# Linear attention and a quick-GELU MLP on one core: the second weight chunk asked for ahead of the casts of k, a later gate, and turns of k moved behind output matmuls

## The chip, the cores and the metric

The kernel runs on one core of a Trainium2 chip. The metric is device time in microseconds (us) of one execution; smaller is better. Engines are named as in the profile: PE multiplies matrices, PEld loads its weights, DVE, ACT and POOL work elementwise, and SP only issues transfers. POOL issues transfers too, in line with its own elementwise work. Sixteen DMA engines carry all transfers.

## The reference

Attention comes first, with a decay `lam[h]` per head, over blocks of 64 positions; its output, with heads side by side, goes through an MLP:

```python
B, H, S, D = 4, 8, 768, 64
for b in range(S // 64):
    intra = einsum('bhic,bhjc->bhij', qb, kb) * Dmask       # lam ** (i - j), lower triangle
    out_b = einsum('bhij,bhjd->bhid', intra, vb) \
          + einsum('bhid,bhde->bhie', qb * lam_pow, kv_state)
    kv_state = lam ** 64 * kv_state + einsum('bhsd,bhse->bhde', kb * rev_pow, vb)
x = out.transpose(0, 2, 1, 3).reshape(3072, 512)
h = x @ w_in                                                # 512 x 2048
return (h / (1 + exp(-1.702 * h))) @ w_out                  # 2048 x 512
```

## The kernel before

The work is cut into six waves of 512 tokens. The first two waves (`w` = 0 and 1) take two batches each and 256 positions of each batch; the other four take all four batches and 128 positions of each. Inside the first two waves a batch is called `c` (0 or 1). This change lies wholly in the first wave, where nothing is in the memory of the core yet and every transfer is just arriving.

For one batch of the first wave the steps are these. `do_cast` (line 195) multiplies k or q, as loaded in float32, by powers of the decay and writes bfloat16; it works in two halves `g` of four heads, of two instructions each, on whichever engine it is given (line 204 of the profile). `turn_pe` (line 234) transposes a half on PE against an identity matrix (line 240) and copies the result out on ACT (line 223) or DVE (line 220). `cast_v` (line 225) casts v. `d_scores` (line 253) multiplies turned q and turned k (line 261), and the products are masked on DVE (line 269) into tiles named sm. `d_one` and `d_state` (line 281) make the running state from k that is not turned and v, `d_keep` (line 291) copies it out. `d_out` (line 310) makes the outputs: masked scores times v into two accumulators, oa and oz (line 318), then q times the state (line 300). `d_x` copies an accumulator to the MLP's input, xT. With xT there, `mlp1_half` (line 408) multiplies two column blocks of the input weight with the tokens of one batch (line 416), and `mlp1` (line 398) one column block with all tokens of the wave (line 404); both end in a GELU on ACT. `fill` issues matmuls of zeros, whose results nobody reads.

The input weight arrives in five chunks of 2, 3, 4, 4 and 3 column blocks of 128 (`IN_CH`, line 173). `load_w_in(j)` (line 180, issued at line 183) asks for chunk j on POOL's queue, converting float32 to bfloat16. In bfloat16 the chunks are 256, 384, 512, 512 and 384 KB. The output weight follows on the same queue in four chunks of 512 KB (`load_w_out`, line 187). The inputs k, q and v go on SP's queue instead (`load_one`, line 79): for batch 0 of the wave in two halves of four heads each, then batch 1 with k and q in halves and v in one piece.

The order of each engine's work is written out by hand: inside `tc.manual_schedule()` (line 686) every engine executes what the program gives it in program order. `gate_pool(x)` (line 680) is a copy of one element of x on POOL: whatever POOL has to do after it waits until x has landed.

The stretch that matters runs from line 695 to line 739: k and q of batch 0 are cast and turned; POOL passes its gate and asks for weight chunk 0; v of batch 0 is cast on ACT; scores of batch 0; POOL casts k of batch 1 and then asks for chunks 1 and 2; the state and output of batch 0 on PE, with the turns of k and q of batch 1 in between; scores of batch 1; the first MLP piece on chunk 0 (line 737), and the state of batch 1. Line 763 finishes batch 1, and the loop at line 764 runs the first MLP pieces that read chunk 1.

Of the kernel before, what the change touches and what calls it, by code (L numbers as in the profile page):

```python
# [25 lines left out]
def kernel(  # L26
# [16 lines left out]
    B, H, S, D = q.shape  # L43
# [33 lines left out]
    loaded = {}  # L77
# [61 lines left out]
    def acc(name, dt=f32, shape=None, tag="a"):  # L139
        return ps.tile(shape or [P, 4, P], dt, tag=tag, bufs={"a": 5, "mm": 3}[tag], name=name)  # L140

    def fill(n, new=None):
        if new:
            fill_ps[0] = acc("ps_fill", shape=[P, W], tag=new)
        for _ in range(n):
            nc.tensor.matmul(fill_ps[0], zero[:, 0:P], zero, start=True, stop=True)
# [33 lines left out]
    def load_w_in(j):  # L180
        c0 = sum(IN_CH[:j]) * P
        t, i = IN_HOME[j]
        nc.gpsimd.dma_start(
            out=w_in_sb[t][:, :, i * P : (i + IN_CH[j]) * P], in_=moe_w_in.rearrange("(kc ki) f -> ki kc f", ki=P)[:, :, c0 : c0 + IN_CH[j] * P])
# [10 lines left out]
    def do_cast(w, c, nm, eng, g=None):  # L195
        if g in (None, 0):
            cast[w, c, nm] = work.tile([P, 2, HD], bf16, tag=f"{nm}s{c}", bufs={"k": 2, "q": 1}[nm], name=f"{nm}s")
        f, x = loaded[w, c, nm], cast[w, c, nm]
        if w < ND:
            pw = {"k": kd_pow, "q": qd_pow}[nm]  # L200
            for R in (0, 1) if g is None else (g,):
                for j in range(2):
                    h = slice(4 * R + 2 * j, 4 * R + 2 * j + 2)
                    eng.tensor_tensor(x.rearrange("p a (r i j d) -> p r j i a d", i=2, j=2, d=D)[:, R, j],  # L204
                                      f[:, h].rearrange("p i (a d) -> p i a d", a=2),
                                      pw[:, h].unsqueeze(3).to_broadcast([P, 2, 2, D]), op=MUL)
        else:
            pw = {"k": k_pow, "q": q_pow}[nm]
            n = 2 * H // 4
            for j in range(2):  # L210
                eng.tensor_tensor(x.rearrange("p b (r i j d) -> p j (b r) i d", i=2, j=2, d=D)[:, j],  # L211
                                  f.rearrange("p h (a d) -> p (h a) d", a=2).rearrange("p (n j i) d -> p j n i d", j=2, i=2)[:, j],
                                  pw.rearrange("p b (r j i) -> p j (b r) i", i=2, j=2)[:, j].unsqueeze(3).to_broadcast([P, n, 2, D]),
                                  op=MUL)
# [10 lines left out]
    def cast_v(w, c, copies=(pool_copy, pool_copy)):  # L225
        f = loaded.pop((w, c, "v"))
        dst = v_sb[w % 2]
        if w < ND:
            for a in range(2):
                copies[a](dst[:, 2 * c + a], f.rearrange("p h (a d) -> p h a d", a=2)[:, :, a, :])  # L230
        else:
            copies[0](dst[:, 2 * c : 2 * c + 2].rearrange("p b h d -> p (b h d)"), f.rearrange("p h e -> p (h e)"))

    def turn_pe(w, c, nm, copy=act_copy, g=None):
        x = cast[w, c, nm]
        rr = list(range(NP)) if g is None else [2 * g, 2 * g + 1]
        t = acc("ps_t", bf16, [P, len(rr), 2, P])
        for i, r in enumerate(rr):
            for a in range(2):
                nc.tensor.transpose(t[:, i, a, :], x[:, a, r * P : (r + 1) * P], ident)  # L240
        if g in (None, 0):
            trans[w, c, nm] = work.tile([P, 2 * NP, P], bf16, tag=f"{nm}T{c}", bufs={"k": 1, "q": 2}[nm], name=f"{nm}T")
        copy(trans[w, c, nm][:, 2 * rr[0] : 2 * rr[0] + 2 * len(rr)], t.rearrange("p r a s -> p (r a) s"))
# [6 lines left out]
    def q_of(w, c, rows, r, blk):  # L250
        return trans[w, c, "q"][rows, 2 * r : 2 * r + 2, D * blk : D * blk + D]
# [34 lines left out]
    def d_one(w, c, tag="a"):  # L286
        states[w, c] = t = acc("ps_kv", shape=[P, NP, D], tag=tag)
        d_state(w, c, t, A)

    def d_keep(w, c):  # L290
        nc.scalar.copy(kv_sb[1][:, 2 * w + c], states[w, c])
        if w:
            kept[w, c] = work.tile([P, NP, D], f32, tag="half", bufs=1, name="half")
            nc.scalar.copy(kept[w, c], states[w, c])

    def d_inter(w, c, t, j, first):
        js, b = (A, Z)[j], 2 * w + c
        for R in range(2):
            for i, cs in enumerate((A, Z)):
                nc.tensor.matmul(t[cs, 2 * R + j, :], kv_sb[1][js, b, 2 * R + i, :], q_of(w, c, js, 2 * R + i, 1),  # L300
                                 start=(first and R == 0), stop=(not first), skip_group_check=True)
# [8 lines left out]
    def d_out(w, c, tags="aa"):  # L310
        vt = v_sb[w % 2]
        oa, old = acc("ps_o", tag=tags[0]), (w, c) in whole
        oz = whole.pop((w, c)) if old else acc("ps_o", tag=tags[1])
        for r in range(NP):
            for a in range(2):
                for t, bs in ((oa, A), (oz, Z)):
                    for i, cs in enumerate((A, Z)):
                        nc.tensor.matmul(t[cs, r, :], vt[bs, 2 * c + a, 2 * r + i, :],
                                         masked[w, c, r // 2, r % 2][bs, i, a, :],
                                         start=(r + a == 0 and (t is oa or not old)),  # L320
                                         stop=(a == 1 and (t is oa or (old and r % 2 == 0))), skip_group_check=True)
        d_inter(w, c, oz, 1, False)
        if w not in xT:
            xT[w] = xp.tile([P, NP, W], bf16, tag="x", name="xT")
        return oa, oz

    def d_x(w, c, i, t, copy):
        n0 = (2 * c + i) * P
        copy(xT[w][:, :, n0 : n0 + P], t)
# [350 lines left out]
    def gate_pool(x):  # L680
        nc.gpsimd.tensor_copy(behind_q, x)  # L681
# [4 lines left out]
    with tc.manual_schedule():  # L686
# [8 lines left out]
        for nm, copies in (("k", (dve_copy, act_copy)), ("q", (act_copy, dve_copy))):  # L695
            for g in range(2):
                do_cast(0, 0, nm, nc.vector, g)
            for g in range(2):
                turn_pe(0, 0, nm, copies[g], g)
                fill({"k0": 2, "q1": 1}.get(f"{nm}{g}", 0))  # L700
        gate_pool(loaded[0, 0, "v"][0:1, 0, 0:1])
        load_w_in(0)
        cast_v(0, 0, (act_copy, act_copy))
        d_scores(0, 0, 0)
        d_scores(0, 0, 1)
        fill(3)
        for g in range(2):
            do_cast(0, 1, "k", nc.gpsimd, g)
        for j in (1, 2):
            load_w_in(j)  # L710
        d_one(0, 0, "mm")
        d_keep(0, 0)
        turn_pe(0, 1, "k", act_copy, 0)
        oa, oz = d_out(0, 0, ("mm", "mm"))
        nc.scalar.copy(seen, oz[:, 3, P - 1 : P])
        d_state(0, 0, states[0, 0], Z)
        do_cast(0, 1, "q", nc.vector, 0)
        do_cast(0, 1, "q", nc.vector, 1)
        turn_pe(0, 1, "k", dve_copy, 1)
        d_x(0, 0, 0, oa, act_copy)  # L720
        turn_pe(0, 1, "q", act_copy, 0)
        d_inter(0, 0, oz, 0, False)
        turn_pe(0, 1, "q", dve_copy, 1)
        d_x(0, 0, 1, oz, act_copy)
        fill(1, "a")
# [164 lines left out]
```

## Time and profile before

| what | us |
|---|---|
| median of 3 runs | 193.13 |
| lowest and highest of the 3 | 191.82, 193.41 |
| the profiled execution, own time | 194.5 |
| its span, first to last instruction | 192.7 |
| PE busy in the span | 185.1 |
| DVE busy | 154.4 |
| ACT busy | 129.8 |
| POOL busy | 53.7 |

PE is busy for nearly all of the span, so what matters is where it is not, and where it runs at a lower clock. Times in the profile count from the first instruction. A row of the timeline reads: start, duration, engine, line, operation, output and inputs, count, and in brackets how long the engine sat idle before it and what ended that. The timeline merges instructions of one kind that follow one another. A row of the chain of waits reads: start, duration, what ran or was waited for. A row of the windows reads: from and to, length, then for each engine its busy time and number of instructions, the clock that PE was granted (1.00 is full), the mean busy share of the DMA engines (over 1 where packets overlap) and GB/s. The transfers of POOL's queue appear as q0, those of SP's as q1.

### The profile page before, as it was taken

What the parts mean: (1) busy time and instruction counts of PE and PEld (TensorE: products, weight loads), DVE (VectorE), ACT (ScalarE), POOL (GpSimd) and SP (SyncE); (2) the same over time, 40 slices, a digit from 0 to 9 for tenths busy, and PEclk for the clock granted to TensorE, in tenths of its full rate; (3) what the DMA queues carried; (4) which work ended last, traced back from release to release, by engine and by line L of the source; (5) the groups of instructions that cost most, each with busy time, mean ns of one, the idle gap of its engine ahead of it and who ended that gap; (6) DMA issues with size and microseconds to landing.
All of it is one profiled execution on the core that took longest, in us unless ns stands there. A gap on an engine that the chain in (4) does not pass through costs nothing.

```text
span 192.7 us, 5553 instructions
## 1 busy us (share of the span) xinstructions
PE 185.1 (96%) x2291; PEld 151.7 (79%) x2293; DVE 154.4 (80%) x296; ACT 129.8 (67%) x243; POOL 53.7 (28%) x78
## 2 busy tenths in 40 slices
PE   7796999999999999999999999999999999999993
PEld 2365644898888888888888888888888888888882
DVE  1896579987586989988799979799879797889850
ACT  4966376145869976479878388878388876587711
POOL 5299000059727000097000195000393000000000
PEclk9999699999999999999999999999999999999999
DMA  5999999999977698989998946999365903300113
GB/s 148 330 249 183 200 204 207 307 297 271 228 187 61 157 236 201 245 217 165 197 241 191 276 113 155 210 250 255 120 163 116 211 8 109 112 3 0 44 51 126
DMA packets 90495, 33.91 MB, mean 176 GB/s; under 512 B 67430, under 2 KB 90470, under 8 KB 90470
## 3 DMA queue, kind: packets, MB, share of 16 engines
q1 hardware_dynamic: 85716, 29.37, 62.2%
q0 software_dynamic: 4752, 4.19, 13.9%
q8 instruction: 18, 0.29, 0.7%
q14 instruction: 7, 0.06, 0.2%
q10 hardware_dynamic: 2, 0.00, 0.0%
HBM read 27.26 MB, written 6.29 MB: 174 GB/s over the span
## 4 chain that ended last, share of the span: by engine, by line
PE 89%; DMA 6%; SPq 2%; POOL 1%; issue 0%; ACT 0%; ACTq 0%; POOLq 0%
PE ps_X L463 18%; PE ps_hX L595 17%; PE ps_V L463 9%; PE ps_hV L595 9%; PE ps_h L404 5%; PE ps_Q L463 5%; PE ps_hQ L595 4%; PE ps_h L416 4%; PE ps_X L513 4%; DMA w_in<-in_moe_w_in_dram 4%; DMA kf<-in_k_dram 3%; PE ps_s L337 2%; PE ps_o L392 2%; SPq L84 2%; PE ps_o L379 1%; POOL ks L204 1%
## 5 line engine op out<-in xcount | busy, mean ns | idle before, releaser
L614 ACT ACTIVATE g_sb<-h_sb 128x512 bf16<-128x512 f32 x57 | 34.5, 632 | 1.2 <-DVE h_sb L603 1.2
L463 PEld LDWEIGHTS <-g_s 128*128 128x128 bf16 x320 | 30.9, 98 | 4.1
L595 PEld LDWEIGHTS <-w_in_t 128*128 128x128 bf16 x304 | 29.7, 98 | 3.6
L223 ACT COPY part<-ps_hX 128x512 f32<-128x512 f32 x34 | 19.5, 586 | 10.4 <-PE ps_hX L595 10.3
L463 PEld LDWEIGHTS <-g_sb 128*128 128x128 bf16 x240 | 22.8, 98 | 3.4
L595 PEld LDWEIGHTS <-w_in 128*128 128x128 bf16 x228 | 22.1, 98 | 2.8
L595 PE MATMUL ps_hX<-x_s,w_in_t 128*128 128x256 bf16 x152 | 22.5, 272 | 0.0
L443 DVE TENSOR_TENSOR g_s<-g_sb 128x1024 bf16<-128x1024 bf16 (+1 forms) x26 | 16.6, 646 | 6.8 <-ACT g_sb L614 5.5
L463 PE MATMUL ps_X<-w_out_t,g_s 128*128 128x256 bf16 x160 | 19.1, 273 | 0.0
L681 POOL CAST behind_q<-x_s 1x1 f32<-1x1 bf16 x4 | 0.7, 174 | 63.5 <-DVE x_s L576 63.5
L211 POOL TENSOR_TENSOR qs<-qf,q_pow 128x512 bf16<-128x512 f32 x16 | 16.3, 1040 | 1.2 <-PE ps_s L261 1.2
L211 POOL TENSOR_TENSOR ks<-kf,k_pow 128x512 bf16<-128x512 f32 x16 | 16.4, 1049 | 0.0
L603 DVE TENSOR_TENSOR h_sb<-part,ps_hX 128x512 f32<-128x512 f32 x19 | 12.9, 681 | 3.9 <-PE ps_hX L595 3.9
L220 DVE COPY part<-ps_hV 128x512 f32<-128x512 f32 x18 | 12.4, 688 | 3.2 <-PE ps_hV L595 3.2
L603 DVE TENSOR_TENSOR h_sb<-part,ps_hV 128x512 f32<-128x512 f32 x19 | 13.0, 684 | 1.0 <-PE ps_hV L595 1.0
L603 DVE TENSOR_TENSOR h_sb<-part,ps_hQ 128x512 f32<-128x512 f32 x19 | 12.9, 681 | 0.4 <-PE ps_hQ L595 0.4
L614 ACT ACTIVATE g_sb<-ps_hX 128x512 bf16<-128x512 f32 x19 | 11.1, 589 | 1.9 <-PE ps_hX L595 1.9
L346 ACT ACTIVATE sm<-ps_s,inv_pow 128x512 bf16<-128x512 f32 x16 | 10.1, 691 | 2.5 <-PE ps_s L337 2.5
L595 PE MATMUL ps_hQ<-xT,w_in 128*128 128x256 bf16 x76 | 11.4, 273 | 0.0
L595 PE MATMUL ps_hV<-x_s,w_in_t 128*128 128x256 bf16 x76 | 11.4, 273 | 0.0
L595 PE MATMUL ps_hV<-xT,w_in_t 128*128 128x256 bf16 x76 | 11.4, 273 | 0.0
L595 PE MATMUL ps_hX<-x_s,w_in 128*128 128x256 bf16 x76 | 11.3, 273 | 0.0
(127 smaller groups left out, 365.2 us busy)
## 6 DMA issues: line engine op xcount, KB each, us to landing
vf<-in_v_dram SPq DMA_DIRECT2D x11, 512.0 KB, 5.7
kf<-in_k_dram SPq DMA_DIRECT2D x10, 512.0 KB, 6.4
qf<-in_q_dram SPq DMA_DIRECT2D x10, 512.0 KB, 6.7
out_dram<-o_sb SPq DMA_DIRECT2D x24, 128.0 KB, 2.4
out_dram<-o_sb SPq DMA_DIRECT2D x12, 256.0 KB, 3.4
w_out<-in_moe_w_out_dram POOLq DMA_DIRECT2D x4, 512.0 KB, 15.3
kf<-in_k_dram SPq DMA_DIRECT2D x4, 256.0 KB, 3.2
qf<-in_q_dram SPq DMA_DIRECT2D x4, 256.0 KB, 4.5
```

Of the source, the lines that this page charges most:

```text
L211: eng.tensor_tensor(x.rearrange("p b (r i j d) -> p j (b r) i d", i=2, j=2, d=D)[:, j], f.rearrange("p h (a d) -> p (h a) d", a=2).rearran ...
L220: nc.vector.tensor_copy(out, in_)
L223: nc.scalar.copy(out, in_)
L346: nc.scalar.activation(sm, s, COPY, scale=inv_pow[:, n : n + 1])
L404: nc.tensor.matmul(h, w_in_sb[j][:, kc, i * P : (i + 1) * P], xT[w][:, kc, :], start=(kc == 0), stop=(kc == KC - 1))
L416: nc.tensor.matmul(h[:, u, :], w_in_sb[j][:, kc, i * P : (i + 1) * P], xT[w][:, kc, cols], start=(kc == 0), stop=(kc == KC - 1))
L443: nc.vector.tensor_tensor(o, x, y, op=f)
L463: nc.tensor.matmul(bank[:, t], x[:, m, t * P : (t + 1) * P], y, start=(n in (1, 2, 7) and t == ts[0] * last and m == 0), stop=(m == FFC // ...
L513: nc.tensor.matmul(bank[:, t], x[:, m, t * P : (t + 1) * P], y, start=(n in (1, 2, 7, 4) and t == 0 and m == 0), stop=(m == FFC // 2 - 1), ...
L595: nc.tensor.matmul(bank[:, u], z[:, kc], y[:, kc], start=(n in (1, 2, 7) and u + kc == 0), stop=(kc == 1), skip_group_check=True)
L603: nc.vector.tensor_tensor(h, h_part[w, g, {2: 1, 5: 7, 4: 6}[n]], bank, op=ADD)
L614: nc.scalar.activation(g_of[w][:, a : b + 1 : b - a, 256 * i : 256 * i + 256], bank, GELU)
```

## The change

Three things change, all of them in the order of instructions; what is computed is the same.

- POOL's gate reads an element of the second half of v of batch 0 (head 4) in place of one of the first half (head 0).
- Behind the gate POOL asks for chunks 0 and 1 in a row. Before, it asked for chunk 0, cast both halves of k of batch 1, and then asked for chunks 1 and 2. Chunk 2 keeps its place.
- The turns of k of batch 1 move later in PE's order. The first half, which stood ahead of the output matmuls of batch 0, now stands behind them and behind the state (`d_state`); in ACT's order its copy stands behind the first `d_x`. The second half moves behind the `d_inter` that follows; DVE's order stays as it was. SP's queue is not touched.

```diff
-        gate_pool(loaded[0, 0, "v"][0:1, 0, 0:1])
-        load_w_in(0)
+        gate_pool(loaded[0, 0, "v"][0:1, H // 2, 0:1])
+        for j in range(2):
+            load_w_in(j)
         cast_v(0, 0, (act_copy, act_copy))
         d_scores(0, 0, 0)
         d_scores(0, 0, 1)
         fill(3)
         for g in range(2):
             do_cast(0, 1, "k", nc.gpsimd, g)
-        for j in (1, 2):
-            load_w_in(j)
+        load_w_in(2)
         d_one(0, 0, "mm")
         d_keep(0, 0)
-        turn_pe(0, 1, "k", act_copy, 0)
         oa, oz = d_out(0, 0, ("mm", "mm"))
         nc.scalar.copy(seen, oz[:, 3, P - 1 : P])
         d_state(0, 0, states[0, 0], Z)
         do_cast(0, 1, "q", nc.vector, 0)
         do_cast(0, 1, "q", nc.vector, 1)
-        turn_pe(0, 1, "k", dve_copy, 1)
         d_x(0, 0, 0, oa, act_copy)
+        turn_pe(0, 1, "k", act_copy, 0)
         turn_pe(0, 1, "q", act_copy, 0)
         d_inter(0, 0, oz, 0, False)
+        turn_pe(0, 1, "k", dve_copy, 1)
         turn_pe(0, 1, "q", dve_copy, 1)
```

## The prediction

> **What bounds the kernel now.** I read the waits of PE first, then the chain of waits, the granted clock by stretches, and last the timeline of the first 19 us. The waits of PE from 17 us to the end hold one row:
>
> ```profile
> PE ps_h L416 <- DMA w_in<-in_moe_w_in_dram: 1.3, 1, 1.3
> ```
>
> PE stops for a transfer once in all that time. The chain of waits shows where that transfer comes from, and a later row the price of the same matmuls elsewhere:
>
> ```profile
> 9.50 2.27 POOL ks L204 x4
> 11.77 6.99 DMA w_in<-in_moe_w_in_dram
> 18.76 0.05 issue
> 18.81 4.46 PE ps_h L416 x24
> ...
> 50.48 0.98 PE ps_h L416 x8
> ```
>
> POOL casts k of batch 1 for 2.27 us; only then, at 11.77, does it ask for chunk 1, which lands at 18.76; the next 24 matmuls need it. Eight of them take 0.98 us at 50.48, so 24 are worth 2.94, yet here they took 4.46. The windows say why:
>
> ```profile
> 5.52:8.93 3.41, 2.41 (x44) 1.41 (x47) 2.76 (x8) 3.00 (x7) 1.06 (x2) 1.00 1.14 343
> 12.35:15.76 3.41, 3.22 (x65) 2.04 (x63) 3.11 (x8) 2.92 (x7) 2.95 (x5) 1.00 1.24 165
> 15.76:19.17 3.41, 2.06 (x76) 1.57 (x73) 1.50 (x4) 2.03 (x7) 3.33 (x6) 1.00 1.21 186
> 19.17:22.58 3.41, 3.41 (x19) 2.35 (x17) 2.53 (x8) 1.05 (x2) 0.00 (x0) 0.50 1.26 205
> 17.54:18.81 1.27, 0.00 (x1) 0.00 (x1) 0.69 (x1) 0.42 (x2) 1.27 (x3) 1.00 1.24 203
> ```
>
> PE does nothing from 17.54 to 18.81 (last row). In the 3.41 us that end at 19.17 it was busy for 2.06, and in the next 3.41 its clock is 0.50. So the wait costs 1.27 us and, if the low clock is its child, 4.46 - 2.94 = 1.52 us more. After 18.81 PE is never idle for long, so a start there that is earlier should reach the end, unless something later is short of time.
>
> **The change, part by part.** First POOL and ACT as they are:
>
> ```profile
> 7.87 0.17 POOL L681 COPY behind_q<-vf 1x1 f32<-1x1 f32 x1 [4.50 <-DMA vf<-in_v_dram]
> 7.99 0.95 POOL L183 DMA_DIRECT2D w_in<-in_moe_w_in_dram  x1
> 8.63 1.14 ACT L223 CAST v_sb<-vf 128x512 bf16<-128x512 f32 x2 [0.37 <-DMA vf<-in_v_dram]
> 9.50 2.32 POOL L204 TENSOR_TENSOR ks<-kf,kd_pow 128x256 bf16<-128x256 f32 x4 [0.56 <-DMA kf<-in_k_dram]
> 11.77 1.55 POOL L183 DMA_DIRECT2D w_in<-in_moe_w_in_dram  x2
> 13.78 0.61 POOL L217 CAST v_sb<-vf 128x512 bf16<-128x512 f32 x1 [0.46 <-DMA vf<-in_v_dram]
> ```
>
> *Gate.* ACT's cast needs all of v and starts at 8.63, so the second half lands at about 8.6; the gate moves by 8.63 - 7.87 = 0.76, chunk 0 is asked for at 8.75 in place of 7.99 and, at 0.95, chunk 1 at 9.7 in place of 11.77: 2.1 us earlier. Behind the gate POOL has both requests and the casts of k, and nobody else waits for POOL.
>
> *Casts of k.* They start when the second request is issued, 9.7 + 0.78 (half of 1.55) = 10.5 in place of 9.50, and end 2.32 later at 12.8 in place of 11.8. Chunk 2 is asked for at 12.8 in place of 12.55, the cast of v (13.78, waiting for its data) keeps its time, and so do the requests behind it.
>
> *Turns of k.* The rows of PE, DVE and ACT that they move past:
>
> ```profile
> 10.73 0.40 PE L240 MATMUL ps_t<-ident,ks 128*128 128x128 bf16 x4 [0.36 <-POOL ks L204]
> 11.39 1.72 DVE L204 TENSOR_TENSOR qs<-qf,qd_pow 128x256 bf16<-128x256 f32 x4
> 12.04 0.59 ACT L223 CAST xT<-ps_o 128x512 bf16<-128x512 f32 x1
> 12.13 0.40 PE L240 MATMUL ps_t<-ident,ks 128*128 128x128 bf16 x4
> 12.49 0.40 PE L240 MATMUL ps_t<-ident,qs 128*128 128x128 bf16 x4
> 12.82 0.30 PE L300 MATMUL ps_o<-qT,kv 64*64 64x128 bf16 x4
> 12.93 0.58 ACT L223 COPY qT<-ps_t 128x512 bf16<-128x512 bf16 x1 [0.29 <-PE ps_t L240]
> 13.71 0.79 PE L261 MATMUL ps_s<-qT,kT 64*64 64x128 bf16 x32
> 14.64 0.77 PEld L416 LDWEIGHTS <-w_in 128*128 128x128 bf16 x8 [0.30 <-DMA w_in<-in_moe_w_in_dram]
> ```
>
> Without the first turn PE may begin the output matmuls earlier, but their last quarter waits for the fourth mask, which DVE ends as the casts of q start (11.39), so they end as before. The first turn takes the place of the second at 12.13 (its k is cast by 10.5 + 1.2 = 11.7), q's first turn stays at 12.49, and the second turn of k, its k cast at 12.8, follows the `d_inter` at 13.1: one turn of some 0.35 now stands where there was a gap of 0.2 for q's casts, so PE reaches the scores 0.25 later, at 13.95. On ACT the copy of k (0.58) follows xT at 12.63, and q's ends at 13.65 in place of 13.5, in time. Scores, masks and all up to the end of batch 1 shift by 0.25, which brings PE's end of batch 1 from 17.54 to 17.8. If the cover fails (POOL 0.3 later, say), it is that much more; at best it is nothing. The first MLP piece starts at 14.9 and must have chunk 0, which landed at 14.6 (PE was held 0.30 for it).
>
> *Chunk 0 and 1 on their way.* POOL's queue and SP's share the engines. Rows of q0 in 1 us stretches from 11, 13, 14 and 22 us, and of all q0 moved by 18.76 (a row reads: packets, MB, share of 16 engines):
>
> ```profile
> q0 software_dynamic: 43, 0.02, 15.9%
> q0 software_dynamic: 240, 0.13, 113.8%
> q0 software_dynamic: 193, 0.14, 113.5%
> q0 software_dynamic: 257, 0.20, 130.0%
> q0 software_dynamic: 1512, 1.12, 42.7%
> ...
> w_in<-in_moe_w_in_dram POOLq DMA_DIRECT2D x1, 256.0 KB, 6.6
> w_in<-in_moe_w_in_dram POOLq DMA_DIRECT2D x1, 384.0 KB, 7.0
> ```
>
> Chunks 0 and 1 are 0.64 MB, but 1.12 MB of q0 had moved when chunk 1 was complete: its last piece was not short of bandwidth, it came late while others went ahead. The queue also dips, to 193 packets in the us in which chunk 1 begins against 257 later. Both look like requests that were not ready when their turn came. Chunk 1 lands, with its own 7.0 from request to landing, at 9.7 + 7.0 = 16.7 at the earliest; if only its turn counts, at 18.76 as now; if chunk 0's later request pushes all back by 0.76, at 19.5. I take any time before 17.8, because of the 1.12 MB. For chunk 0 the ends are 14.6 (its turn behind SP's packets, unchanged) and 15.4 (0.76 later); I take 14.6, within the 0.25 by which PE comes later. The Trainium skill (DMA: Bandwidth & Descriptors, Issuing engines are not separate DMA queues) says that transfers asked for by different engines run on the same 16 DMA engines and interleave, so that asking early saves only issue time; by that, chunk 1 stays at 18.76 and the 1.27 shrinks only by what PE comes later.
>
> *Low clock.* With chunk 1 there, PE runs through from 17.8 and no stretch is as idle as 2.06 busy of 3.41; the first row of the windows, 2.41 of 3.41, was not followed by a low clock. I take the 1.52 as saved; the ends are 0 and 1.52. The Trainium skill (TensorE: Matmul & The Clock Gate, Part 1) has the clock follow PE's activity over a free-running window of about 3.4 us; the 3.41 us at 0.50 agree in length. It also warns of idle gaps over 3.4 us, and here 1.27 us sufficed, so on that point the trace differs.
>
> *What is late next.* PE would be 18.81 - 17.8 = 1.0 and 1.52, together 2.5 us, ahead at 23 us. Later work depends on the output weight, whose transfers do not come earlier for a free PE:
>
> ```profile
> 29.00:39.00 10.00, 10.00 (x73) 6.95 (x72) 9.59 (x26) 3.67 (x7) 0.00 (x0) 1.00 1.16 259
> ...
> 15.80 2.98 POOL L187 DMA_DIRECT2D w_out<-in_moe_w_out_dram  x4
> ...
> DMA to landing us min/median/max: 12.5/15.3/18.1
> ...
> 29.45 0.75 DVE L430 TENSOR_TENSOR w_out_t<-w_out 128x512 bf16<-128x512 bf16 x2
> ...
> 36.60 0.88 DVE L430 TENSOR_TENSOR w_out_t<-w_out,w_out_t 128x512 bf16<-128x512 bf16 x2
> ...
> 38.27 0.60 PE L513 MATMUL ps_W<-w_out_t,g_sb 128*128 128x256 bf16 x4
> ```
>
> DVE is full from 29 to 39 (9.59 of 10). Its first sums of the output weight (29.45) cannot start before that chunk lands, 15.80 + 12.5 = 28.3: DVE gains 1.15 at most. PE's use at 38.27 of what DVE ends at 36.60 + 0.88 = 37.48 has 0.8 to spare. So about 1.95 of the 2.5 passes; a smoother queue may bring the weights a little sooner (0 to 0.5, I take 0.15). The sum is 2.1: 194.5 - 2.1 = 192.4 for an execution like the profiled one. The median, 193.13, is 1.4 below that execution; taken from it, the forecast is 191.0. One of the three runs, 191.82, is 1.3 below the median, about the 1.52 of the low clock: possibly a run without it, which would leave less to gain there.
>
> **Rivals.**
>
> *Its turn, not its request, sets chunk 1.* For it: q0 is over 100% busy in each of the last three stretches, with requests queued. Against it: the 1.12 MB. PE then waits from 17.8 to between 18.3 and 18.76. With 0.5 to 0.95 idle in place of 1.27, the low clock probably goes: 1.52 and 0 to 0.5 saved. Without the low clock 191.1 to 191.6, with it 192.6 to 193.1; middle 191.7.
>
> *The low clock stays though chunk 1 is early.* The stage's matmuls are small (64x64), and if those count for little, 15.76 to 19.17 is idle in any case. Against it: the stretch from 12.35 holds the same small matmuls, 3.22 busy, and was followed by 1.00. Then only 1.0 is saved: 192.1.
>
> *Slower: chunk 0 becomes the wait.* Chunk 0's request is 0.76 later, and PE was already held 0.30 for it. From a landing at 14.9 on PE pays; at 15.4 it stops for 0.5, and chunk 1 behind it lands at 19.5, 0.7 later than now. With two stops a low clock can come twice: 193.13 + 0.7 + 1.5 = 195.3, without the second 193.8. Against it: SP's packets were ahead of chunk 0 anyway; q0 moves 43 packets from 11 to 12 us, three us and more after its request at 7.99, so it was not the request that was late.
>
> **How the numbers follow.** Differences under 1% (1.93 us) are about what a measurement of this kernel cannot tell from no change. Chances: 0.42 for the forecast (191.0, own range 190.4 to 191.6), of which 0.27 fall below 191.2; 0.30 for the turn of chunk 1, of which 0.10 fall below 191.2, since without the low clock its row begins at 191.1; 0.13 for the low clock that stays (0.02 below); 0.15 for chunk 0, of which 0.09 take a second low clock and exceed 195.06 (1% above). That makes faster 0.39, same 0.52, slower 0.09. The range, 190.3 to 193.6, goes from the forecast with the full 2.5 and a little more to the rivals with a low clock, and leaves out the late chunk 0.
>
> **What would show it.** Right: chunk 1 asked for at 9.7 and landed before 17.8; no wait of PE for w_in at 17.8; clock 1.00 throughout 17 to 24 us; 24 matmuls of line 416 in 3 us; the scores of batch 1 at 13.95; PE short waits for w_out_t near 36 us. Wrong: a wait of PE for w_in over 0.5 us at 14.9 or at 18 us, a 0.50 in the clock row after it, or casts of k that end after 13.1.

## The result, and the profile after

| | before | changed |
|---|---|---|
| median of 22 runs each, us | 193.08 | 193.75 |
| lowest and highest | 191.82, 196.14 | 192.09, 195.51 |
| profiled execution, own time | 194.5 | 192.84 |
| its span | 192.7 | 191.1 |

Changed over before is 1.0054, interval 1.0029 to 1.008: about 1.0 us longer, where 2.1 us shorter was forecast. This ratio and those below leave out executions more than 1.5% over the fastest of their kernel. The profiled executions say the opposite, 1.6 us less span after. So one of the two profiles, or both, does not show the ordinary execution, and that is the thread to follow.

The timeline after, with the rows that answer to those of before: POOL's gate, requests and casts of k, the casts of q on DVE, the scores, and PE's first and next 24 matmuls on the weight.

```profile
8.35 0.17 POOL L681 COPY behind_q<-vf 1x1 f32<-1x1 f32 x1 [4.97 <-DMA vf<-in_v_dram]
8.47 1.70 POOL L183 DMA_DIRECT2D w_in<-in_moe_w_in_dram  x2
10.17 2.54 POOL L204 TENSOR_TENSOR ks<-kf,kd_pow 128x256 bf16<-128x256 f32 x4
11.27 3.25 DVE L204 TENSOR_TENSOR qs<-qf,qd_pow 128x256 bf16<-128x256 f32 x4
12.65 0.81 POOL L183 DMA_DIRECT2D w_in<-in_moe_w_in_dram  x1
13.46 0.77 POOL L217 CAST v_sb<-vf 128x512 bf16<-128x512 f32 x1
15.12 0.79 PE L261 MATMUL ps_s<-qT,kT 64*64 64x128 bf16 x32
15.84 1.05 PE L416 MATMUL ps_h<-xT,w_in 128*128 128x256 bf16 x8
18.86 2.84 PE L416 MATMUL ps_h<-xT,w_in 128*128 128x256 bf16 x24
```

POOL does what was worked out, some 0.3 us earlier: requests at 8.47 and 9.4, casts of k at 10.17. But DVE's four casts of q take 3.25 us where they took 1.72, and the scores start at 15.12 instead of 13.71. The 24 matmuls begin at 18.86, no earlier than the 18.81 of before, though chunk 1 was there long since. The requests of chunk 0 and of chunk 1, from the DMA view (the last number is us from request to landing):

```profile
w_in<-in_moe_w_in_dram POOLq DMA_DIRECT2D x1, 256.0 KB, 7.3
...
w_in<-in_moe_w_in_dram POOLq DMA_DIRECT2D x1, 384.0 KB, 7.8
```

Chunk 1 landed at 9.4 + 7.8 = 17.2; chunk 0 at 8.47 + 7.3 = 15.8, 1.2 later than before and just as PE came for it. The waits of PE after 8 us (a row reads: us in total, times, longest):

```profile
PE ps_t L240 <- DVE qs L204: 1.5, 3, 0.6
PE ps_o L318 <- DVE sm L269: 0.6, 2, 0.3
PE ps_fill L146 <- issue: 0.2, 1, 0.2
```

The wait for the transfer is gone, and waits for DVE have come. In this execution the clock stayed at 1.00, also behind the pauses (rows of windows as in the prediction):

```profile
12.35:15.76 3.41, 2.05 (x49) 1.39 (x49) 3.10 (x6) 1.90 (x5) 3.41 (x6) 1.00 1.35 202
15.76:19.17 3.41, 3.33 (x95) 2.43 (x84) 2.05 (x5) 3.23 (x9) 3.19 (x5) 1.00 1.23 201
```

But that is not the rule. Of the 22 runs of the changed kernel 17 had a mean granted clock of 0.982 to 0.991 (0.988 or more in 16 of them), with a median of 194.05, and 5 had 0.998 to 1.000, with a median of 192.93. The profile above is one of the 5.

### The profile page after: what moved, and what is told of

Its sections match the earlier page's. It is cut to its first block, busy times and chain, and to the rows that moved or that the text cites. A ratio compares the mean times of both kernels' runs of the same rounds, so it can differ in the third digit from the quotient of the medians.

```text
span 191.1 us, 5552 instructions
## 1 busy us (share of the span) xinstructions
PE 183.5 (96%) x2290; PEld 150.8 (79%) x2293; DVE 155.4 (81%) x296; ACT 129.7 (68%) x243; POOL 54.0 (28%) x78
## 4 chain that ended last, share of the span: by engine, by line
PE 92%; DVE 5%; ACT 1%; issue 0%; ACTq 0%; DVEq 0%
PE ps_X L463 19%; PE ps_hX L595 18%; PE ps_V L463 9%; PE ps_hV L595 9%; PE ps_h L404 5%; PE ps_Q L463 5%; PE ps_hQ L595 4%; PE ps_h L416 4%; PE ps_X L513 4%; DVE qs L204 2%; PE ps_s L337 2%; PE ps_o L392 2%; PE ps_t L240 1%; DVE sm L269 1%; PE ps_o L379 1%; PE ps_s L261 1%
## 5 line engine op out<-in xcount | busy, mean ns | idle before, releaser
L211 POOL TENSOR_TENSOR qs<-qf,q_pow 128x512 bf16<-128x512 f32 x16 | 16.3, 1040 | 1.7 <-DMA qf<-in_q_dram 1.7
```

## The experiments

Theory A: the casts of k on POOL come later and now meet the casts of q on DVE, and the two slow one another; the later scores are the loss. Theory B: the later or bunched requests are. Theory C: the moved turns are. Theory S: the wait in the first profile of before is rare, so there was little to gain. Theory H: pauses of PE between 10 and 15 us bring the low clock, and that is the loss. "Low" below is an execution with a mean granted clock under 0.995; the others are called executions at full clock. Times such as "scores at 13.77" are starts in the profiled execution of that kernel. Ratios are to the kernel before on the same chip; two executions of 238 and 652 us are left out of the counts.

**Each part alone.** Kernel e1_gate:

```diff
-        gate_pool(loaded[0, 0, "v"][0:1, 0, 0:1])
+        gate_pool(loaded[0, 0, "v"][0:1, H // 2, 0:1])
```

> The gate alone, on the second half of v; requests and turns as before. Theory A (what costs is that POOL casts k of batch 1 while DVE casts q of batch 1, which makes DVE's four casts of q take 3.2 us instead of 1.7): the gate moves chunk 0's request by 0.4 to 0.8 us, POOL's casts of k start at 9.5 to 9.6 as before, since they wait for k at 9.35, DVE's casts of q stay at 1.7 us, and the time stays within 0.3% of before. Theory B (what costs is the later request of chunk 0): chunk 0 lands up to 0.8 later, PE stops for it at 14.7, and the time is 0.3 to 0.5% longer.

Ratio 0.999, interval 0.9954 to 1.0026; low in 1 of 11. Requests at 8.57 and 11.81, casts of k at 9.54, scores at 13.77. Chunk 0 landed at 14.3, no later than before, and PE did not stop for it. The later gate alone costs nothing that shows: B is out for the later request of chunk 0.

Kernel e2_request:

```diff
         gate_pool(loaded[0, 0, "v"][0:1, 0, 0:1])
-        load_w_in(0)
+        for j in range(2):
+            load_w_in(j)
...
-        for j in (1, 2):
-            load_w_in(j)
+        load_w_in(2)
```

> Chunks 0 and 1 asked for in a row at 8.0 and 8.9, with the old gate and the old turns. Theory A: POOL's casts of k run from 9.8 to 12.1 and overlap only the first one or two of DVE's casts of q, which take 1.9 to 2.4 us together instead of 1.7 (3.2 in the changed kernel); chunk 1 lands before 17.5, PE has no wait for it, and the time is 0.3 to 0.7% shorter than before. Theory B (the order of requests itself costs, since chunk 1 competes with k, q and v): v of batch 1 lands later than 13.7, and the time is as in the changed kernel or 0.3% over before.

Ratio 1.0019, 0.998 to 1.0058; low in 1 of 12. In the profiled execution everything on SP's queue was 0.5 late, so the requests went out at 8.50 and 9.44 and the casts ran from 10.20 to 12.54. Scores at 14.43; chunk 1 landed at 17.6. The gain that A expected did not come, though no wait for chunk 1 was left.

Kernel e3_turns moves the turns of k as in the change, and nothing else.

> The turns of k alone moved behind the output matmuls; gate and requests as before. Theory A: casts do not move, DVE's casts of q stay at 1.7 us, PE reaches the scores of batch 1 at 13.7 to 14.0 (0 to 0.25 later), and the time is within 0.2% of before. Theory C (the moved turns are what costs): scores at 14.5 or later, and the time is 0.4% or more above before.

Ratio 1.0016, 0.9975 to 1.0058; low in 1 of 12. Scores at 13.75, as A has it, where C had 14.5 or later: the moved turns alone do not delay PE. The interval by itself does not exclude the 0.4% of C. Chunk 1 (asked for at 11.70) landed after 5.4 us, at 17.1.

Kernel e4_old_gate is the changed kernel without the later gate, that is e2 and e3 together.

> The changed kernel with the gate back on the first half of v. Theory A: POOL's casts of k run from 9.8 to 12.1 instead of 10.2 to 12.7, so that less of DVE's casts of q is doubled: 2.0 to 2.6 us instead of 3.2; scores of batch 1 at 14.0 to 14.5 instead of 15.1; the time is 0.3 to 0.6% below the changed kernel. Theory B (the later gate only delays chunk 0): chunk 0 lands earlier, the scores stay at 15.1, and the time is as in the changed kernel.

Ratio 1.0016, 0.9974 to 1.0057; low in 4 of 12. Casts of k from 9.95, one cast of q of four lengthened (2.15 us in all), scores at 14.85. Three of the four low executions took 196.35 to 197.35 and are not in the ratio; no profile shows one of them. The fourth is the profiled one. It shows the low clock early (rows of windows):

```profile
10.23:13.64 3.41, 2.48 (x80) 1.79 (x78) 3.35 (x7) 1.78 (x5) 2.80 (x5) 1.00 1.20 265
13.64:17.05 3.41, 3.41 (x47) 2.41 (x46) 2.36 (x5) 2.31 (x5) 2.99 (x5) 0.50 1.31 205
```

**Casts that meet.** Kernel e5_late_casts, on the kernel before:

```diff
+        idle = op.tile([P, 2, W], bf16, tag="o", name="idle")
+        nc.gpsimd.memset(idle, 0.0)
         for g in range(2):
             do_cast(0, 1, "k", nc.gpsimd, g)
```

> The kernel before, with one extra fill of a spare tile on POOL between chunk 0's request and the casts of k of batch 1, so that these start about 0.6 us later (10.1 instead of 9.5); requests of chunks 1 and 2 follow the casts, as before, and are later too. What it leaves unchanged: the turns and the gate. Theory A (the changed kernel loses because POOL's casts of k come later and fall on DVE's casts of q): DVE's casts of q take 1.9 us or more instead of 1.7, the scores of batch 1 start 0.4 to 1.0 us later than the 13.7 of before, and the time is 0.2 to 0.6% over before. Theory B (it loses through order of requests or turns): scores at 13.7 to 13.9 and the time within 0.2% of before.

Ratio 1.0029, 0.999 to 1.0068. The fill was short: casts of k moved by 0.2 only, to 9.70. Casts of q 1.93 us, scores at 13.93. PE also waited 0.5 us for chunk 1, which is asked for behind the casts and so 0.2 later. The result fits A for so small a step, but it tells little.

Kernel e6_k_half_dve, on the changed kernel:

```diff
-        for g in range(2):
-            do_cast(0, 1, "k", nc.gpsimd, g)
+        do_cast(0, 1, "k", nc.gpsimd, 0)
...
         do_cast(0, 1, "q", nc.vector, 0)
+        do_cast(0, 1, "k", nc.vector, 1)
         do_cast(0, 1, "q", nc.vector, 1)
```

> The changed kernel, with the second half of k of batch 1 cast on DVE between the two halves of q, and only the first on POOL. Theory A (POOL and DVE slow one another when both cast from memory): DVE has six casts instead of four and yet is done by 14.0, since at most one or two meet POOL's; POOL is free for chunk 2's request at 11.4 instead of 12.7; scores at 14.2 to 14.7 instead of 15.1, and the time 0 to 0.4% below the changed kernel. If the casts do not disturb each other: six casts at 0.83 take 5.0 us, scores after 16.5, and the time is 0.7% over the changed kernel.

Groups by tile of line 204: in the changed kernel (first two rows), and in e6:

```profile
L204 POOL TENSOR_TENSOR ks<-kf,kd_pow x4: 632/642/818, 10.2 to 11.9; 128x256 bf16<-128x256 f32 x4
L204 DVE TENSOR_TENSOR qs<-qf,qd_pow x4: 826/840/969, 11.3 to 13.7; 128x256 bf16<-128x256 f32 x4
```

```profile
L204 DVE TENSOR_TENSOR qs<-qf,qd_pow x4: 410/410/483, 11.3 to 13.0; 128x256 bf16<-128x256 f32 x4
L204 POOL TENSOR_TENSOR ks<-kf,kd_pow x2: 627/630/633, 10.3 to 10.8; 128x256 bf16<-128x256 f32 x2
L204 DVE TENSOR_TENSOR ks<-kf,kd_pow x2: 410/410/411, 12.0 to 12.4; 128x256 bf16<-128x256 f32 x2
```

Median ns of one cast on DVE: 840 beside POOL, 410 apart from it. Six casts are done by 13.4 where four took until 14.5, and the scores start at 14.03. This part of A is shown. Yet the next matmuls did not come sooner:

```profile
PE ps_h L416 <- DMA w_in<-in_moe_w_in_dram: 1.0, 1, 1.0
```

PE waited 1.0 us for chunk 0, which landed at 15.8 as in the changed kernel. Ratio 1.0024, 0.9989 to 1.0059; low in 2 of 12.

**The changed kernel on another chip.** Kernel e8_changed_again, no edit:

> The changed kernel once more, beside the others on one chip, for a second profile. Theory A: casts of k on POOL start at 10.1 to 10.3 and overlap the casts of q on DVE, which take 2.1 us or more; scores at 14.4 to 15.2; chunk 1 in time; 0.3 to 0.8% over before. Rival: the first profile showed a rare case; casts of q in 1.7 us, scores at 14.0, and the time within 0.2% of before.

Ratio 1.0035, 0.9991 to 1.0078. Low in 7 of 12, with a median of 194.32; the other 5 had 192.91. The kernel before was low in 2 of 29 there, and the other 27 had 192.81. At full clock the two kernels are thus 0.1 us apart (5 executions against 27, which range from 191.49 to 194.51). The casts of k started at 10.80, later than A has it, the casts of q took 2.52 us, and the scores started at 14.99. That the scores are 1.3 later and the time at full clock is the same speaks against the later scores as the net loss, and for the clock.

**A gate still earlier.** Kernel e7_gate_q is e2 with the gate on q:

```diff
-        gate_pool(loaded[0, 0, "v"][0:1, 0, 0:1])
+        gate_pool(loaded[0, 0, "q"][0:1, H // 2, 0:1])
```

> Chunks 0 and 1 asked for in a row, but behind a gate on the second half of q of batch 0, which lands at 7.1, so that both requests are out before k of batch 1 lands at 9.35; turns as before. Theory A: casts of k at 9.5 to 11.8 and casts of q in 1.7 us, as before; scores at 13.7; chunk 1 lands by 17.2 in every execution; the time is that of before where chunk 1 was in time there, and up to 1 us less where it was not: 0 to 0.4% below before. Theory D (weights asked for early take bandwidth from v and from k of batch 1): k of batch 1 lands later than 9.7 and scores start later than 14.0: 0.2% or more above before.

Ratio 1.0315, 1.0261 to 1.0369; low in all 6. It was above all v of batch 1 that paid: here chunk 0 was asked for at 7.95, ahead of v at 8.45.

```profile
7.95 1.70 POOL L183 DMA_DIRECT2D w_in<-in_moe_w_in_dram  x2
...
8.45 0.69 SPq L84 DMA_DIRECT2D vf<-in_v_dram  x1
...
18.26 0.60 POOL L217 CAST v_sb<-vf 128x512 bf16<-128x512 f32 x1 [5.23 <-DMA vf<-in_v_dram]
```

v landed at 18.2 instead of 13.7, and PE stood 2.3 us for its cast. Theory D, which named v and k, fits. Its signs for k came too (k at 9.9, scores at 14.83), but they prove less: in this execution SP's requests were 0.5 late, as in e2.

**Is the wait of before the rule?** Kernel f1_before_again, no edit:

> The kernel before once more, for a second profile. Theory S (the late last piece of chunk 1 in the first profile of before, and the 1.27 us for which PE waited for it, are rare): chunk 1 lands at 16.5 to 17.5, PE reaches the 24 matmuls of line 416 at 17.5 without a wait for it, clock 1.00 there, span 189.5 to 190.8. Rival (the wait is the rule): chunk 1 at 18.2 or later, a wait of 0.7 us or more, span 191.5 or more.

Chunk 1 landed at 17.9, between the two expectations; span 191.0, clock 1.00. Its waits of PE:

```profile
PE ps_W L513 <- DVE w_out_t L430: 0.6, 1, 0.6
PE ps_h L416 <- DMA w_in<-in_moe_w_in_dram: 0.4, 1, 0.4
```

With chunk 1 asked for at 11.70 to 11.81 the wait was 1.27 in the first profile, 0.4 here, and 0 in e1 and e3, where chunk 1 landed at 17.0 and 17.1. So its size differs from execution to execution, and S is not settled by four profiles. And PE, 2.5 us earlier here at the last of the 24 matmuls (it starts at 20.46 against 23.00), waits 0.6 us at 36 us for the sums of the output weight.

**Pauses filled.** Kernel f2_fills, on the changed kernel (the fill that stands ahead of the scores then writes to the same tile):

```diff
+        fill(2, "a")
         oa, oz = d_out(0, 0, ("mm", "mm"))
...
+        fill(2)
         turn_pe(0, 1, "q", act_copy, 0)
...
+        fill(2)
         turn_pe(0, 1, "q", dve_copy, 1)
```

> The changed kernel with six more matmuls of zeros on PE in the pauses that it has: two ahead of the output matmuls of batch 0, two ahead of each turn of q of batch 1. Theory H (a large part of the loss is a low clock that follows PE's pauses between 10 and 15 us, in more than half of the executions): granted clock under 0.995 in at most 3 of 12 runs, against 7 of 12 of the changed kernel on the last chip, and the time 0.2 to 0.6% below the changed kernel, within 0.3% of before. Rival (the low clock does not come from these pauses): as often as in the changed kernel, and the time the same as there or up to 0.3 us more.

Low in 0 of 12, as H has it. But the time is 1.0046, 1.0017 to 1.0074, which is a miss. In its profile the scores start at 15.61 and the last of the 24 matmuls at 21.9, later than in the three profiles of the changed kernel at full clock, and PE has a wait near 95 us that they do not have, for a transposing transfer of q:

```profile
PE ps_s L337 <- DMA qT<-qs: 0.8, 1, 0.8
```

The same wait stands in the profiles of e5 (1.1), e7 (0.8) and e4 (0.5). Whether it comes in every execution of f2 is not known, so this run leaves open how much of the loss is the clock's.

Kernel f3_gate_request: later gate and bunched requests, old turns.

> The changed kernel with the turns of k back in their old places: later gate and chunks 0 and 1 in a row. Theory A (the later casts of k cost, wherever the turns stand): PE now waits for the first half of k at 10.7 to 11.4, the casts of q overlap POOL's and take 2.1 to 3.2 us, scores at 14.4 to 15.2, and the time is that of the changed kernel or up to 0.3% more: the moved turns save something once the casts are late. Rival C (the moved turns cost): 0.3% or more below the changed kernel and within 0.2% of before.

Ratio 1.002, 0.9984 to 1.0055; low in 2 of 12. PE waits 1.3 us for the first half of k, scores at 14.93. The interval does not tell the two outcomes apart. The few low executions do say something: with the turns in their old places, the late casts of k alone seldom bring the low clock.

Kernel f4_half_old_gate is e6 with the old gate.

> The changed kernel with the old gate, and with the second half of k of batch 1 cast on DVE: no cast of POOL meets more than one of DVE, and chunk 0 is asked for at 8.0. Theory A with chunk 0 (the loss is the doubled casts first and, where these are gone, the late last piece of chunk 0): scores at 13.9 to 14.3, chunk 0 by 15.0, the first matmuls of line 416 at 14.8 to 15.1, chunk 1 by 17.3 and no wait for it; the time within 0.2% of before and 0.2% or more below the changed kernel. If chunk 0 is late whatever the gate: it lands at 15.5 or later, PE waits for it 0.5 us or more, and the time is as in the kernel with the later gate and the same casts, 0.2% over before.

Ratio 1.0015, 0.9978 to 1.0053; low in 4 of 12. Three of the four took 196.09 to 196.47 and are not in the ratio. The profiled one of these, with a span of 194.3, had v of batch 1 land at 18.3, with chunk 0 and v asked for within 0.01 us of one another. Chunk 0 landed at 16.3 and PE waited 1.0 us for it, as the second expectation has it, but with v late as well the run does not settle what delays chunk 0. The low clock of this execution begins at 19.42, behind 1.6 us in which PE waits for v's cast.

**Where the low clock lies.** Kernels g1_changed_third and g2_changed_fourth, no edit:

> The changed kernel, for a third profile. Theory H (pauses of PE between 10 and 15 us bring the low clock): if the granted clock is under 0.995, the 0.50 lies in the 3.4 us that begin somewhere from 12 to 17 us, right behind the pauses, and span is 192.3 or more; at full clock the span is 190.4 to 191.6. Rival (the low clock comes behind chunk 1, as in the first profile of the kernel before): the 0.50 begins at 18.5 or later.

> The changed kernel, for a fourth profile, with the same expectations as for the third: with the low clock, 0.50 in the 3.4 us that begin between 12 and 17 us by theory H, at 18.5 or later by the rival; span 192.3 or more with it, 190.4 to 191.6 without.

g1 ran at full clock (0.998, span 191.0, scores at 14.94). g2 was low (0.991), with a span of 191.8, under the 192.3 that was expected with the low clock:

```profile
9.67:13.09 3.42, 2.27 (x74) 1.51 (x72) 3.42 (x7) 1.47 (x4) 3.41 (x6) 1.00 1.23 289
13.09:16.50 3.41, 3.00 (x48) 2.15 (x49) 2.55 (x5) 1.31 (x4) 3.41 (x6) 0.50 1.29 200
```

The low clock begins at 13.09, behind 3.42 us in which PE was busy for 2.27: where H put it, and not behind chunk 1. It is the only low execution of the changed kernel itself of which there is a profile.

Kernel g3_fewer_fills, on the changed kernel:

```diff
+        fill(2, "a")
         turn_pe(0, 1, "q", act_copy, 0)
...
+        fill(2)
         turn_pe(0, 1, "q", dve_copy, 1)
         d_x(0, 0, 1, oz, act_copy)
-        fill(1, "a")
```

> The changed kernel with two matmuls of zeros ahead of each turn of q of batch 1 (and one fewer ahead of the scores), and none ahead of the output matmuls. Theory H: granted clock under 0.995 in at most 3 of 12 executions; scores not later than in the changed kernel (15.0 to 15.3); time 0.2 to 0.5% below the changed kernel's, 0 to 0.3% over before. Rival (pauses at the turns do not bring it): low clock in 6 or more of 12 and the changed kernel's time, 0.35 to 0.55% over before.

Ratio 1.0000, 0.997 to 1.0031; low in 0 of 12. The same stretches as in g2:

```profile
9.67:13.09 3.42, 2.76 (x77) 1.72 (x77) 3.42 (x7) 1.47 (x4) 3.42 (x6) 1.00 1.24 307
13.09:16.50 3.41, 3.11 (x57) 2.05 (x57) 3.25 (x7) 2.31 (x6) 3.41 (x6) 1.00 1.31 204
```

Its casts of q are as slow as in the changed kernel (0.79 to 0.84 each) and its scores start at 14.83; what it lacks is the pauses at the turns of q, and the loss is gone. That is the strongest single result for H. The counts (0 of 12 against 25 of 36 of the changed kernel) are clear of chance. The times are less so: this interval still overlaps that of e8.

**Asking for chunk 1 earlier without casts that meet.** Kernel g4_half_before, on the kernel before: POOL casts the first half of k, then asks for chunks 1 and 2; DVE casts the second half.

```diff
-        for g in range(2):
-            do_cast(0, 1, "k", nc.gpsimd, g)
+        do_cast(0, 1, "k", nc.gpsimd, 0)
...
         do_cast(0, 1, "q", nc.vector, 0)
+        do_cast(0, 1, "k", nc.vector, 1)
         do_cast(0, 1, "q", nc.vector, 1)
-        turn_pe(0, 1, "k", dve_copy, 1)
         d_x(0, 0, 0, oa, act_copy)
         turn_pe(0, 1, "q", act_copy, 0)
         d_inter(0, 0, oz, 0, False)
+        turn_pe(0, 1, "k", dve_copy, 1)
```

> The kernel before, with the old gate and chunk 1 asked for behind POOL's casts of the first half of k only, at 10.7 instead of 11.8; the second half of k is cast on DVE between the halves of q, and turned behind the first turn of q. Theory A: DVE's six casts are done by 13.5, scores at 13.9 to 14.1 (0.3 later than before), chunk 1 lands by 17.2, no wait for it, and the time is within 0.2% of before. If asking 1.1 us earlier is worth what the first profile promised: 0.5% or more below before.

Ratio 0.9994, 0.996 to 1.0029; low in 0 of 12; chunk 1 was asked for at 10.54 and landed at 17.1; PE did not wait for it, and the scores started at 13.98. All is as A has it, and worth nothing that can be measured. No version was measurably faster than the kernel before.

## Why the prediction was wrong

*"The 1.52 as saved": the step that failed most.* The low clock of before was taken for a standing cost. On the four chips of the experiments the kernel before was low in 1 of 34, 2 of 29, 3 of 29 and 3 of 23 executions, 9 of 115; the changed kernel, in all its runs, in 17 of 22, 7 of 12, 0 of 1 and 1 of 1, 25 of 36. The profile of before that the prediction read was one of the rare low ones. The prediction noted that the fastest of the three runs was "possibly a run without it", and took the 1.52 all the same. Low executions of the changed kernel took 194.05 - 192.93 = 1.1 us more in the first set and 194.32 - 192.91 = 1.4 in the second. Weighted with 25/36 - 9/115 = 0.62 that is, as an estimate, 0.7 to 0.9 us of the 1.0 us lost. The change does not remove a low clock, it brings one, by the pauses that it opens at the turns of q: filled, they no longer bring it (g3). Whether the pause ahead of the output matmuls, where a turn of k stood before, adds to it was not tested by itself. The low clock comes often only with both the moved turns and casts that meet: the moved turns alone (e3) were low in 1 of 12, late casts with the old turns (f3) in 2 of 12, moved turns with casts that hardly meet (e6) in 2 of 12, and bunched requests and moved turns without the later gate (e4) in 4 of 12. What speaks against the clock as the whole loss is f2, at full clock in all 12 and still 0.46% over.

*"PE reaches the scores 0.25 later".* The scores came at 15.12, 14.99, 14.94 and 15.60 in four profiles, 1.2 to 1.9 later than 13.71. This ate what the missing wait gave: the 24 matmuls began at 18.86, not at 17.8. The step that failed is the price of the casts of q, in which the cost of meeting POOL was put at nothing. They were priced at 1.72 from a row in which three of four had POOL's casts behind them; the first, that did meet one, is the 714 ns among the least, median and greatest time (410, 413 and 714 ns) of these casts in the profile of before. The Trainium skill (SBUF — State Buffer, SBUF: two separate sides) says that VectorE and GpSimd share a pair of ports, held for a whole instruction, when the VectorE instruction has two inputs from SBUF and GpSimd's reads SBUF too. The casts of q have two, and 840 ns beside POOL against 410 apart agrees.

*"The wait costs 1.27".* One execution's wait was read as the rule; f1 had 0.4, e1 and e3 none. The 1.12 MB that had moved by then, read as a sign of late requests, are no such sign: when chunk 1 was complete, 0.84 MB had moved in e1 and e3 and 1.01 in the changed kernel. Nor do the profiles show that asking earlier brings chunk 1 earlier. Asked for at 9.40, 10.04, 9.97 and 9.47 in the four profiles of the changed kernel, it landed at 17.2, 17.8, 17.1 and 18.0; asked for at 11.77, 11.79, 11.81 and 11.70 (before, f1, e1, e3) it landed at 18.8, 17.9, 17.0 and 17.1. That the first profile has it "before 17.8" is luck as far as these eight show. The rival by which its turn and not its request sets chunk 1 fits them better, though its landing at 18.76 was that of one execution. PE no longer waits because chunk 1 is there by 18.0 and PE, held up by the later scores, comes at 18.7 to 19.6.

*"Chunk 0 ... I take 14.6".* It landed at 15.8; PE met that without a wait there, but waited 0.5 us in e8 and 1.0 in e6. The rival on chunk 0 was right that it can come late, but its reason is not shown: with the later request alone (e1) it landed at 14.3, and with both requests in a row anywhere from 14.1 (g3) to 16.3 (e8, g2). Nor does it decide: e8 at full clock took no longer than before.

*"What is late next"* held in part. It let a piece of the gain be lost behind the output weight, and f1 shows such a wait (0.6 us at 36 us), e1 a smaller one (0.3), e3 and g4 none. Otherwise what PE wins or loses before 23 us reaches the end. In the sixteen profiles other than e7 and f4, take the end of the 24 matmuls from the span. This leaves 169.4 to 169.6 us in eleven, whether the 24 end at 20.34 (e3), at 22.40 (g2) or at 23.27 (the first profile of before). The other five have 0.3 to 1.3 more, nearly all of it one later wait of PE: that for the output weight in e1 and f1, that for a transposing transfer of q in e4, e5 and f2. So the later scores do cost. That the kernels are still equal at full clock suggests that the kernel before loses about as much in waits that come in some of its executions, such as those of its two profiles.

*Open.* What the clock counts: in the first profile of the changed kernel 2.05 of 3.41 us busy was followed by 1.00, in g2 2.27 of 3.42 by 0.50, and in e4 even 2.48 of 3.41, so busy time alone does not decide; the place of the stretch or the kind of matmul counts too. The Trainium skill (TensorE: Matmul & The Clock Gate, Part 1) says that the window runs freely and does not start with the kernel; e4 and g2 agree. In e4 the granted clock falls at 13.64 and, behind the last matmul, again at 191.13, which is 52 times 3.413 us later; in g2 it falls at 13.09. That this phase decides which execution of a kernel is low is not shown. Open too is why a chunk lands late in some executions, and what makes full-clock executions of the kernel before differ by 3 us (191.49 to 194.51 beside e8), where the five of e8 differ by 1.1.

## What to carry to other kernels

Look at more than one execution before a wait or a low clock is taken for a cost: the wait that this change set out to remove was 1.27, 0.4, 0 and 0 us in four profiles in which chunk 1 was asked for at the same time. Nor did asking 2 us earlier bring the chunk earlier (17.1 to 18.0 against 17.0 to 18.8, four profiles each), so see whether a landing follows its request before work is moved to make the request earlier. When work moves on one engine, write down what the other engines do in its new place; a cast on POOL beside a cast on DVE doubled the latter. And a turn that is moved away leaves a pause: two matmuls of zeros in each of the two pauses took the low clock from 25 of 36 executions to 0 of 12, and the ratio from 1.0054 and 1.0035 to 1.0000.

## What the runs showed that was not expected

- A request of SP's queue that is made behind two of POOL's can be served behind them: v of batch 1 landed at 13.7 when asked for 0.01 us before chunk 0 (7.98 and 7.99, in before) and at 18.2 when asked for 0.5 us after it (e7). The price was 3.15% (interval 2.61 to 3.69). Starts as close as 0.01 us do not tell the order: with the same 0.01 v landed at 18.3 in f4.
- Each low clock that a profile shows between PE's matmuls lasted 3.4 us, at 0.50, wherever it began (13.09 in g2, 13.64 in e4, 19.17 in the first profile of before, 19.42 in f4, 21.16 in e7).
- A cast of POOL beside DVE's suffers too, but less: 642 ns median and up to 818 in the changed kernel, against 602 in the kernel before.
